# Window attention, max layer and gated layer: operand sums moved to VectorE, a raw-weight buffer and a new list order

## The chip, the cores and the metric

One core of a Trainium2 chip runs the whole program. The metric is the device time of one execution in microseconds. A core has five engines that run side by side, each through its own queue and in that queue's order: TensorE (PE, with its weight load PEld), VectorE (DVE), ScalarE (ACT), GpSimd (POOL) and SyncE (SP), which here issues nearly all DMA transfers.

## What is computed

Attention over a window of 32 with 32 global tokens, then a layer that takes the maximum of three products, then a gated layer; 2176 tokens of width 512 go through the two layers. The part that the change touches, cut:

```python
def _moe_ref(x, w1, w2, w3, w_out):                 # 512 -> 768 -> 512
    h = np.maximum(np.maximum(x @ w1, x @ w2), x @ w3)
    return h @ w_out

def _moe2_ref(x, w_gate, w_val, w_out):             # 512 -> 1536 -> 512
    gate = 1.0 / (1.0 + np.exp(-(x @ w_gate)))
    val = x @ w_val
    return gate * val @ w_out
```

The weights arrive as float64 and are converted on the chip from raw 32-bit halves.

## The kernel before

All SBUF work is laid out by hand and every step is a generator: one call of it issues one or a few instructions on given engines. `put` and `once` enter the steps with a nominal time into the list `ev`; `ORDER`, a list of numbers written out in the file, says in which order they are called. The order in which steps are called is the order of each engine's queue, and waits between engines follow from which memory a step reads and writes.

The stages overlap. Attention runs in 32 units up to about 400 us; the max layer ("first layer") runs in eight chunks of 256 or 288 tokens (`moe1_l1`, blocks f of the hidden width, three weights each, and `moe1_l2`), the last chunk, number 7, at 404 to 454 us, with its blocks in the order 2, 1, 0, 4, 3, 5. A hidden block needs a max by VectorE, a cast by ScalarE and the difference `h` by GpSimd (`sub`, line 269).

The gated layer multiplies by Strassen's scheme in its Winograd form: a *unit* (q, j, p) is gate or value (q = 0, 1), weight block j of six, token pair p of three; it has seven products (`l3_prod`, line 1021) of six matmuls, and 384 or 320 columns. Each operand is split in a high part (cast by ScalarE) and a low part (difference). `x_prep(p)` makes the seven token operands of a pair, `w_prep(q, j)` the seven weight operands of a block from raw columns: ScalarE and VectorE convert (`to_f32`, lines 283 to 292; 289 and 292 are VectorE's two conversion steps), then four sums (lines 984 to 992) and three differences (997, 1000, 1002). These sums and differences run on GpSimd for 8 of the 12 weight blocks, and 4 of 7 differences of `x_prep` (line 964) do, too. The products of one unit accumulate in the banks `pa`, `pb` and `pe`; between products ScalarE must copy the bank `pa` to `sn` (`snap`, line 1027) before PE may go on in it, so a snapshot that is late stops PE. `l3_out` then adds (line 1040, one operand in PSUM), applies the sigmoid or multiplies (line 1046, both operands in SBUF), and SP stores to `gd`.

PE runs a unit's products in the order 1, 5, 4 of the unit before, 6, 2, 3 of the unit before, 7. `wo_pre` converts `w_out` and stores it; `wo_prep(f)` loads and splits one block of it (lines 1068 to 1074), `g_prep(i)` loads and splits 128 tokens of the gated result (1082 to 1089), `moe2_l4` (1100) is the output product, `moe2_out` evicts and stores it.

Raw columns of weights go through two places, `AWR` and `AWR2`, which `w_prep` and `wo_pre` share. The first layer's weights lie in 26 slots of 4 KB a partition; when that layer has used them, slots 0 to 3.5 become the gated layer's first weight buffer, 3.5 to 7 the second, and 7 to 17.5 hold token pair 1.

Of the kernel before, what the change touches and what calls it, by code (L numbers as in the profile page):

```python
# [190 lines left out]
]  # L191

SLOT = {
# [9 lines left out]
def kernel(  # L203
# [61 lines left out]
    def f32(ap):  # L265
        return ap.bitcast(F32)
# [1049 lines left out]
```

## Time and profile before

| | |
|---|---|
| median of 3 runs | 863.91 us (862.85 to 868.32) |
| profiled execution | 865.5 us, span 863.8 us, mean granted clock 0.99 |
| PE / PEld busy | 95% / 87% of the span |
| DVE / ACT / POOL busy | 60% / 52% / 29% |
| chain that ended last | PE 71%, DVE 8%, DMA 8%, SP queue 5%, issue 4%, ACT 3%, POOL 1% |
| DMA | 109.73 MB, mean 127 GB/s |

The span is the time from the first to the last instruction of the profiled execution; its own time is 1.7 us longer. "Busy" is the time in which an engine executes; matmuls are pipelined, and their ends are modelled. Times in rows are from the start of the span.

### The profile page before, as it was taken

Reading aid. Unit: us, or ns where it says so; the run is one execution under the profiler, and the core shown is the slowest. Engines: PE = TensorE matmul, PEld = TensorE weight load, DVE = VectorE, ACT = ScalarE, POOL = GpSimd, SP = SyncE. Lnnn points to the kernel's source line nnn. Section 1 sums busy time; section 2 is a strip of 40 time slices with the busy share of each in tenths; the row PEclk is TensorE's granted clock in tenths of the full one; section 3 lists DMA queues with packets and bytes.
Section 4 is the critical chain, followed back from the end, with each engine's and each line's share of the span. In section 5 each row is a group of like instructions: output and inputs, shape, how many; then the busy total and the mean of one; then the engine's idle time right before and its main releaser. Section 6 shows DMA issues by size and latency. Waiting matters only on the chain.

```text
span 863.8 us, 17113 instructions
## 1 busy us (share of the span) xinstructions
PE 823.5 (95%) x6422; PEld 747.3 (87%) x6422; DVE 516.8 (60%) x1126; ACT 448.4 (52%) x1100; POOL 252.4 (29%) x223
## 2 busy tenths in 40 slices
PE   5899699999999999999998999999999999999998
PEld 3677589898998989899898999999999988888886
DVE  3969867757666576853776765667665557122120
ACT  4986456736555575563446645656564435222221
POOL 2142245234232433422542131544444012000000
PEclk9999799999999999999999999999999999999999
DMA  8967346444445455455223245536342157443430
GB/s 201 269 173 194 80 78 116 82 91 98 97 102 94 79 112 108 86 86 158 74 100 123 95 156 175 195 127 226 136 149 83 58 189 226 132 143 114 130 110 36
DMA packets 224707, 109.73 MB, mean 127 GB/s; under 512 B 160752, under 2 KB 209392, under 8 KB 224624
## 3 DMA queue, kind: packets, MB, share of 16 engines
q1 hardware_dynamic: 221968, 107.98, 46.7%
q8 instruction: 50, 0.82, 0.4%
q10 hardware_dynamic: 2656, 0.66, 0.4%
q14 instruction: 33, 0.27, 0.1%
HBM read 71.76 MB, written 25.43 MB: 113 GB/s over the span
## 4 chain that ended last, share of the span: by engine, by line
PE 71%; DVE 8%; DMA 8%; SPq 5%; issue 4%; ACT 3%; POOL 1%; DVEq 0%; ACTq 0%; POOLq 0%
PE acc L1100 16%; PE pa L1021 12%; PE ps L319 9%; PE ps L321 8%; PE ps L320 8%; PE pe L1021 5%; DMA m<-in_moe_w_dram 4%; PE pb L1021 3%; PE sp L611 2%; PE ot L765 2%; PE ps L903 2%; PE sg L628 1%; DVE m L292 1%; DVE m L289 1%; DMA m<-gd 1%
## 5 line engine op out<-in xcount | busy, mean ns | idle before, releaser
L1021 PE MATMUL pa<-m,m 128*128 128x384 f32 (+1 forms) x864 | 158.6, 331 | 10.2 <-ACT sn L1027 10.0
L1021 PEld LDWEIGHTS pa<-m,m 128*128 128x128 f32 x864 | 144.8, 189 | 15.2 <-ACT sn L1027 14.9
L319 PE MATMUL ps<-xt,m 128*128 128x288 f32 (+1 forms) x504 | 149.3, 296 | 3.1 <-DVE h L881 3.1
L321 PE MATMUL ps<-xt,m 128*128 128x288 f32 (+1 forms) x504 | 146.6, 291 | 0.0
L320 PE MATMUL ps<-xt,m 128*128 128x288 f32 (+1 forms) x504 | 145.0, 288 | 0.0
L1100 PE MATMUL acc<-m,m 128*128 128x512 f32 x612 | 139.1, 389 | 0.0
L1100 PEld LDWEIGHTS acc<-m,m 128*128 128x128 f32 x612 | 114.8, 188 | 23.8
L319 PEld LDWEIGHTS ps<-xt,m 128*128 128x128 f32 x504 | 94.7, 188 | 11.1 <-issue 4.5
L320 PEld LDWEIGHTS ps<-xt,m 128*128 128x128 f32 x504 | 94.8, 188 | 0.0
L321 PEld LDWEIGHTS ps<-xt,m 128*128 128x128 f32 x504 | 94.7, 188 | 0.0
L1089 DVE TENSOR_TENSOR m<-m,m 128x768 fp32r<-128x768 f32 x34 | 32.1, 977 | 90.0 <-ACT m L1087 89.9
L1021 PE MATMUL pe<-m,m 128*128 128x384 f32 (+1 forms) x432 | 83.1, 327 | 0.0
L1027 ACT COPY sn<-pa 128x384 f32<-128x384 f32 (+1 forms) x108 | 49.2, 458 | 58.3 <-PE pa L1021 53.5
L1021 PEld LDWEIGHTS pe<-m,m 128*128 128x128 f32 x432 | 73.2, 189 | 0.0
L881 DVE TENSOR_TENSOR h<-ps,h 128x288 f32<-128x288 f32 (+1 forms) x90 | 39.1, 437 | 53.2 <-PE ps L321 45.7
L646 ACT ACTIVATE sm<-sm,st 128x224 f32<-128x224 f32 x128 | 60.7, 477 | 9.6 <-DVE st L617 9.3
L1105 ACT COPY o<-acc 128x512 f32<-128x512 f32 x17 | 10.0, 587 | 102.5 <-issue 74.0
L269 POOL TENSOR_TENSOR h<-h,h 128x288 fp32r<-128x288 f32 (+1 forms) x42 | 37.0, 883 | 83.6 <-ACT h L886 78.0
L692 DVE TENSOR_TENSOR pc<-sm,pc 64x512 f16<-64x512 f32 (+1 forms) x72 | 51.5, 715 | 6.5 <-ACT pc L689 5.6
L269 POOL TENSOR_TENSOR m<-m,m 128x512 fp32r<-128x512 f32 x24 | 33.1, 1384 | 72.2 <-ACT m L310 46.3
L585 POOL TENSOR_TENSOR vr<-vr,vb 128x512 f32<-128x512 f32 x24 | 29.9, 1246 | 80.4 <-ACT vb L583 66.0
L617 DVE CUSTOM_DVE_ANT_0 sm<-sp,mask 128x224 f32<-128x224 f32 x128 | 43.8, 383 | 13.2 <-PE sp L611 10.6
(158 smaller groups left out, 1580.8 us busy)
## 6 DMA issues: line engine op xcount, KB each, us to landing
m<-gd SPq DMA_DIRECT2D x17, 768.0 KB, 4.9
m<-in_moe_w_dram SPq DMA_DIRECT2D x18, 512.0 KB, 6.2
gd<-sgt SPq DMA_DIRECT2D x48, 192.0 KB, 3.4
m<-in_moe_w_gate_dram SPq DMA_DIRECT2D x6, 1024.0 KB, 5.8
m<-in_moe_w_val_dram SPq DMA_DIRECT2D x6, 1024.0 KB, 6.0
m<-in_moe_w_out_dram SPq DMA_DIRECT2D x6, 1024.0 KB, 5.2
vr<-in_v_l_dram SPq DMA_DIRECT2D x48, 96.0 KB, 2.5
out_dram<-o SPq DMA_DIRECT2D x17, 256.0 KB, 2.0
```

The costliest lines, as they stand in the source:

```text
L269: nc.gpsimd.tensor_tensor(out=out, in0=a, in1=f32(b), op=ALU.subtract)
L319: nc.tensor.matmul(ps, lhsT=wh, rhs=xh, start=first, stop=False)
L320: nc.tensor.matmul(ps, lhsT=wh, rhs=xl, start=False, stop=False)
L321: nc.tensor.matmul(ps, lhsT=wl, rhs=xh, start=False, stop=last)
L617: nc.vector.tensor_tensor_reduce(out=sm[:, hh, j], in0=sp[hh][:, j, 0:224], in1=mask[:, half + j, :], scale=-SC, scalar=3.0e38, op0=ALU.ad ...
L646: nc.scalar.activation(sm4[:, i], sm4[:, i], AF.Exp, bias=st[:, 0, i:i + 1], scale=-1.0, accum_out=st[:, 2, i:i + 1])
L692: nc.vector.tensor_tensor(out=l_, in0=s_, in1=h_, op=ALU.subtract)
L881: nc.vector.tensor_tensor(out=a, in0=ps[:, 0:n], in1=a, op=ALU.max)
L1021: nc.tensor.matmul(ps, lhsT=w[l][:, a, i], rhs=x[m][:, i], start=(k in (1, 2, 5) and i + l + m == 0), stop=(k in (2, 3, 4) and i == 1 and ...
L1027: nc.scalar.copy(t[:, 0:n], pend[u]["a"][:, 0:n])
L1089: nc.vector.tensor_tensor(out=lo, in0=a, in1=f32(hi), op=ALU.subtract)
L1100: nc.tensor.matmul(acc[i], lhsT=t[l][:, f % 6], rhs=w[m], start=(f == 0 and l + m == 0), stop=(f == NF2 - 1 and l == 1))
```

## The change

- `x_prep`, `w_prep` and `wo_prep`: all sums and differences go to VectorE; GpSimd keeps those of the first layer.
- `w_prep`: the cast of the four sums is issued in two halves.
- A third place for raw columns: a tile `wr` in the pool that holds `sgt`. `wo_pre` and the block (0, 1) use it; `AWR` and `AWR2` are then left to the other blocks.
- `SLOT`: the slots of `w` and `raw` of the first layer are permuted. Each group of tenants that shared a slot still shares one: blocks 2, 1, 0 now lie in slots 0 to 2, 3 to 5, 6 to 8, blocks 4, 3, 5 in 9 to 11, 12 to 14, 15 to 17.
- `tm` has two buffers in place of three; the output tile `o` lies where the weight buffers were.
- `ORDER` and the nominal times: the first 1918 entries, up to the last chunk's first product, name the same steps; from there the list is new. It has 24 more entries, two for each `w_prep`. In it `x_prep(0)` runs ahead of the conversion of the first gate block; the loads of `wo_prep` are issued one by one during the units (1, 5, 0) and (1, 5, 1), where they stood behind the former's last product; the load of gate block 2 is issued before those of `x_prep(2)`; and `g_prep`'s first casts stand after product 4 of unit (0, 5, 2).

The diff without the lists:

```diff
 SLOT: ("kx", 1): 11 -> 14, ("vrg", 0, 0): 7 -> 1
-SLOT.update({("raw", i): n for i, n in enumerate(
-    (9, 8, 21, 2, 10, 1, 19, 13, 17, 12, 23, 14, 16, 15, 18, 20, 25, 24, 6, 13, 17, 12, 23, 21))})
-SLOT.update({("w", i): i for i in range(24)})
+for k, n in (("raw", (12, 2, 21, 8, 13, 7, 19, 10, 17, 9, 23, 11, 16, 15, 18, 20, 25, 24, 0, 10, 17, 9, 23, 21)),
+             ("w", (6, 7, 8, 3, 4, 5, 0, 1, 2, 12, 13, 14, 9, 10, 11, 15, 16, 17, 18, 19, 20, 21, 22, 23))):
+    SLOT.update({(k, i): s for i, s in enumerate(n)})
...
 x_prep
-            eng = nc.gpsimd if op in (B11, T2, T3, B22) else nc.vector
-            eng.tensor_tensor(out=v[1], in0=a, in1=f32(v[0]), op=ALU.subtract)
+            nc.vector.tensor_tensor(out=v[1], in0=a, in1=f32(v[0]), op=ALU.subtract)
...
-    def w_prep(q, j, buf, at, fast):
+    def w_prep(q, j, buf, at):
-        raw = mem(at, (KD * 2 * P, 2), I32)
+        if at:
+            raw = mem(at, (KD * 2 * P, 2), I32)
+        else:
+            raw = sg_pool.tile([P, KD * 2 * P, 2], I32, tag="wr", name="wr", bufs=1)
...
-        eng = nc.vector if fast else nc.gpsimd
-        tt = eng.tensor_tensor
+        tt = nc.vector.tensor_tensor
...
-        nc.scalar.copy(hi[:, S1:S4 + 1], lo)
-        yield
+        for o in (0, 2):
+            nc.scalar.copy(hi[:, S1 + o:S1 + o + 2], lo[:, o:o + 2])
+            yield
...
 l3_out
-            c = d if q == 0 else rb.tile([P, CH], F32, tag="tm", name="tm", bufs=3)[:, 0:n]
+            c = d if q == 0 else rb.tile([P, CH], F32, tag="tm", name="tm", bufs=2)[:, 0:n]
 wo_pre
-        raw = mem(at, (2 * DM, 2), I32)
+        raw = sg_pool.tile([P, 2 * DM, 2], I32, tag="wr", name="wr", bufs=1)
 wo_prep
-        (nc.gpsimd if f % 2 else nc.vector).tensor_tensor(out=lo, in0=v, in1=f32(hi), op=ALU.subtract)
+        nc.vector.tensor_tensor(out=lo, in0=v, in1=f32(hi), op=ALU.subtract)
 moe2_out
-        o = rb.tile([P, DM], F32, tag="o", name="o", bufs=3)
+        o = mem(DM * (i % 3), (DM,))
...
-    jobs = [(0, 0, 0, AWR, T_ATT + .1, 424.0), (1, 0, 1, AWR, 429.5, 0), (0, 1, 0, AWR, 458.0, ended[(0, 0, 2), 3] + .3)]
-    free = {AWR: ended[(0, 0, 2), 3] + 8.5, AWR2: 466.0}
+    jobs = [(0, 0, 0, AWR, T_ATT + .2, 0), (1, 0, 1, AWR, 421.5, 0), (0, 1, 0, 0, 456.0, ended[(0, 0, 2), 3] + .3)]
+    free = {AWR: 458.0, AWR2: 466.0}
```

## Rows read from the trace of the kernel before

**Rows 1.** busy time by stretch: length, each engine (instructions), granted clock, DMA share, GB/s

```profile
420.00:454.00 34.00, 31.46 (x229) 30.79 (x230) 24.90 (x30) 15.45 (x28) 15.58 (x11) 1.00 0.28 95
454.00:500.00 46.00, 42.21 (x238) 40.63 (x238) 33.70 (x49) 27.67 (x51) 9.09 (x5) 0.96 0.32 107
...
542.00:584.00 42.00, 41.70 (x251) 41.07 (x251) 27.64 (x39) 25.43 (x44) 22.50 (x17) 1.00 0.50 170
...
710.00:732.00 22.00, 19.66 (x94) 16.99 (x93) 15.25 (x20) 12.47 (x23) 6.29 (x5) 0.92 0.78 254
...
sum 464.00, PE 447.02 PEld 416.84 DVE 236.80 ACT 205.38 POOL 114.74; mean PE 44.70 PEld 41.68 DVE 23.68 ACT 20.54 POOL 11.47
```

**Rows 2.** TensorE's waits from 400 us: total, times, longest, us

```profile
PE pa L1021 <- ACT sn L1027: 10.0, 12, 2.0
PE ps L319 <- DVE h L881: 2.1, 2, 2.0
PE ps L320 <- POOL h L269: 0.7, 1, 0.7
```

**Rows 3.** busy time around two stretches at a low clock, columns as in rows 1

```profile
458.00:462.00 4.00, 3.93 (x14) 3.93 (x14) 2.14 (x1) 1.78 (x3) 1.05 (x1) 0.57 0.41 107
462.00:470.00 8.00, 8.00 (x48) 8.00 (x48) 4.84 (x6) 3.95 (x8) 1.98 (x1) 1.00 0.79 279
700.00:709.00 9.00, 9.00 (x59) 9.00 (x58) 5.95 (x11) 3.81 (x8) 1.82 (x2) 1.00 0.82 246
713.00:719.00 6.00, 5.57 (x26) 5.05 (x25) 3.69 (x7) 4.24 (x10) 2.32 (x2) 0.72 1.09 367
```

**Rows 4.** groups of VectorE by shape, 400 to 732: count | busy, mean ns | idle before

```profile
L1046 DVE TENSOR_TENSOR sgt<-tm,sgt 128x384 f32<-128x384 f32 x36 | 30.1, 835 | 1.0
L292 DVE SCALAR_TENSOR_TENSOR m<-m 128x1024 int32<-128x1024 int32 x18 | 26.4, 1464 | 0.1
L289 DVE SCALAR_TENSOR_TENSOR m<-m 128x1024 int32<-128x1024 int32 x18 | 25.2, 1398 | 10.0 <-ACT m L287 9.9
...
L997 DVE TENSOR_TENSOR m<-m,m 128x512 fp32r<-128x512 f32 x4 | 2.8, 692 | 2.7 <-ACT m L994 2.7
...
L992 DVE TENSOR_TENSOR m<-m,m 128x256 f32<-128x256 f32 x4 | 1.7, 418 | 0.0
```

**Rows 5.** single VectorE instructions: duration ns min/median/max, first and last start

```profile
L289 DVE SCALAR_TENSOR_TENSOR m<-m x18: 1217/1227/3190, 415.8 to 657.7; 128x1024 int32<-128x1024 int32 x18
...
L1046 DVE TENSOR_TENSOR sgt<-tm,sgt x54: 485/559/2127, 478.3 to 730.9; 128x384 f32<-128x384 f32 x36, 128x320 f32<-128x320 f32 x18
L1040 DVE TENSOR_TENSOR tm<-pe,sn x36: 482/546/560, 481.0 to 729.6; 128x384 f32<-128x384 f32 x24, 128x320 f32<-128x320 f32 x12
```

**Rows 6.** groups of GpSimd by shape, 400 to 732, columns as in rows 4, one group

```profile
L269 POOL TENSOR_TENSOR h<-h,h 128x288 fp32r<-128x288 f32 x6 | 5.6, 926 | 13.9 <-ACT h L886 8.4 <-issue 5.5
```

**Rows 7.** timeline at 513 us: start, length, engine and line, idle before

```profile
513.25 2.40 POOL L1002 TENSOR_TENSOR m<-m,m 128x1024 fp32r<-128x1024 f32 x1
...
513.54 3.19 DVE L289 SCALAR_TENSOR_TENSOR m<-m 128x1024 int32<-128x1024 int32 x1 [4.87 <-ACT m L287]
...
518.64 1.14 PE L1021 MATMUL pa<-m,m 128*128 128x384 f32 x5 [1.65 <-ACT sn L1027]
```

**Rows 8.** timeline at 417 us of VectorE and TensorE

```profile
417.52 2.75 DVE L292 SCALAR_TENSOR_TENSOR m<-m 128x1024 int32<-128x1024 int32 x1
420.19 0.95 DVE L964 TENSOR_TENSOR m<-m,m 128x768 fp32r<-128x768 f32 x1
...
419.32 0.28 PE L321 MATMUL ps<-h,m 128*128 128x256 f32 x1
421.56 0.40 PE L319 MATMUL ps<-xt,m 128*128 128x288 f32 x1 [1.97 <-DVE h L881]
```

**Rows 9.** timeline at 711 us of ScalarE and TensorE

```profile
711.26 0.83 ACT L1087 CAST m<-m 128x768 fp32r<-128x768 f32 x1 [2.86 <-DMA m<-gd]
...
712.47 1.15 PE L1021 MATMUL pa<-m,m 128*128 128x320 f32 x6 [1.91 <-ACT sn L1027]
```

More of the change, by code (lines that the diff above doesn't have):

```diff
@@ L113 @@
     1740, 1225, 1294, 1226, 1737, 1739, 1295, 1296, 1297, 1298, 1308, 1309, 1729, 1750, 1310, 1311, 1741, 1742, 1312,
[77 rows of a table removed]
[78 rows of a table added]
 ]
 SLOT = {
-    ("qn", 0): 15, ("kx", 0): 25, ("kn", 0): 22, ("qn", 1): 20, ("kx", 1): 11, ("kn", 1): 18, ("vrg", 0, 0): 7,
+    ("qn", 0): 15, ("kx", 0): 25, ("kn", 0): 22, ("qn", 1): 20, ("kx", 1): 14, ("kn", 1): 18, ("vrg", 0, 0): 1,
     ("vrg", 0, 4): 4, ("vrg", 1, 0): 24, ("vrg", 1, 4): 22,
 }
-SLOT.update({("raw", i): n for i, n in enumerate(
-    (9, 8, 21, 2, 10, 1, 19, 13, 17, 12, 23, 14, 16, 15, 18, 20, 25, 24, 6, 13, 17, 12, 23, 21))})
-SLOT.update({("w", i): i for i in range(24)})
+for k, n in (("raw", (12, 2, 21, 8, 13, 7, 19, 10, 17, 9, 23, 11, 16, 15, 18, 20, 25, 24, 0, 10, 17, 9, 23, 21)),
+             ("w", (6, 7, 8, 3, 4, 5, 0, 1, 2, 12, 13, 14, 9, 10, 11, 15, 16, 17, 18, 19, 20, 21, 22, 23))):
+    SLOT.update({(k, i): s for i, s in enumerate(n)})
 @with_exitstack
@@ L993, in w_prep @@
         yield
-        nc.scalar.copy(hi[:, S1:S4 + 1], lo)
-        yield
+        for o in (0, 2):
+            nc.scalar.copy(hi[:, S1 + o:S1 + o + 2], lo[:, o:o + 2])
+            yield
         low = mem(3584 * buf + 1792, (7, 2, P), F32R)
+        w7[q, j] = hi, low
         tt(out=low[:, A11:A12 + 1].rearrange("p o k f -> p (o k) f"), in0=h[:, :, 0],
@@ L1002, in w_prep @@
         tt(out=low[:, S1:S4 + 1], in0=lo, in1=f32(hi[:, S1:S4 + 1]), op=ALU.subtract)
-        w7[q, j] = hi, low
         yield
@@ L1051, with wo_pre @@
     wo = {}
-    def wo_pre(i, at):
-        raw = mem(at, (2 * DM, 2), I32)
+    def wo_pre(i):
+        raw = sg_pool.tile([P, 2 * DM, 2], I32, tag="wr", name="wr", bufs=1)
         nc.sync.dma_start(out=raw.rearrange("p (f d) t -> p f (d t)", f=2),
@@ L1059, in wo_pre @@
         yield from to_f32(raw, True, out=c)
-        c = f32(c)
         yield
-        nc.sync.dma_start(out=wod[2 * i:2 * i + 2].rearrange("f p d -> p f d"), in_=c.rearrange("p (f d) -> p f d", f=2))
+        nc.sync.dma_start(out=wod[2 * i:2 * i + 2].rearrange("f p d -> p f d"), in_=f32(c).rearrange("p (f d) -> p f d", f=2))
         yield
@@ L1195, in end_moe1 @@
     def end_moe1():
-        nonlocal sgt
+        nonlocal sgt, sg_pool
         xh_x.close()
@@ L1200, in end_moe1 @@
         post.append(sg_x)
-    rb = sgt = ps_b = None
+    rb = sgt = sg_pool = ps_b = None
     post = []
@@ L1236 @@
         for f, t, t0 in ((0, 0, ended[v, 2] + .25), (1, 1, ended[v, 7] + .7), (0, 1, ended[v, 3] + .25)):
-            put(("l3o", *v, f, t), steps(t0, 0, .7, 1.5), l3_out(v, f, t))
+            put(("l3o", *v, f, t), steps(t0, 0, .7 if v[0] else 1.5, 1.5), l3_out(v, f, t))
         put(("l3o", *v, 1, 0), steps(ended[v, 4], .2, 1.5), l3_out(v, 1, 0))
-    for p, tm in ((0, T_ATT + .2), (1, 426.0), (2, 450.8)):
-        first = (7.0, 7.0, 3.5)[p]
-        put(("xp", p), steps(tm, 0, first, *(3 * (.8,)), *(14 * (.6 if p == 2 else .8,))), x_prep(p))
+    for p, tm, first in ((0, T_ATT + .3, 8.5), (1, 424.0, 8.0), (2, 450.8, 3.5)):
+        put(("xp", p), steps(tm, 0, first, *(3 * (1.25 if p == 1 else .9,)), *(14 * (.6 if p == 2 else .8,))), x_prep(p))
     AWR2 = AXR
-    jobs = [(0, 0, 0, AWR, T_ATT + .1, 424.0), (1, 0, 1, AWR, 429.5, 0), (0, 1, 0, AWR, 458.0, ended[(0, 0, 2), 3] + .3)]
-    free = {AWR: ended[(0, 0, 2), 3] + 8.5, AWR2: 466.0}
+    jobs = [(0, 0, 0, AWR, T_ATT + .2, 0), (1, 0, 1, AWR, 421.5, 0), (0, 1, 0, 0, 456.0, ended[(0, 0, 2), 3] + .3)]
+    free = {AWR: 458.0, AWR2: 466.0}
     for n in range(3, 2 * (NF2 // 2)):
@@ L1249 @@
         jobs.append((q, j, q, AWR2 if n % 2 else AWR, None, ended[(q, j - 1, 2), 3] + .3))
-    n_wo = 0
     for q, j, buf, place, t0, ready in jobs:
@@ L1253 @@
             t0 = free[place]
-            if (q, j) != (1, 1) and n_wo < NF2 // 2:
-                put(("wo", n_wo), steps(t0, 0, 9.0, 1.2, 1.2, 1.3, 1.3), wo_pre(n_wo, place))
-                n_wo += 1
-                t0 += 15.5
-            free[place] = ready + 8.5
-        fast = (q, j) in ((0, 1), (1, NF2 // 2 - 1)) or j == 0
-        first = steps(t0, 0, 9.0, 1.2, 1.2, 1.3)
-        gaps = (.1, .4, .4, .4, .4, .4, .6, .4) if fast else (.1, .7, .7, .7, .7, .7, 1.3, .7)
-        put(("w7", q, j), first + steps(max(ready, first[-1] + 1.2), *gaps), w_prep(q, j, buf, place, fast))
-    assert n_wo == NF2 // 2
+        first = steps(t0, 0, 9.0, 1.2, 1.2, 1.3)
+        go = max(ready, first[-1] + 1.4)
+        if j > 1 or (q, j) == (1, 1):
+            free[place] = go + 7.5
+        put(("w7", q, j), first + steps(go, *(.1, .45, .45, .45, .45, .6, .6, .8, .6, 1.2)), w_prep(q, j, buf, place))
+    for i in range(NF2 // 2):
+        put(("wo", i), steps(490.0 + 28 * i, 0, 9.0, 1.2, 1.2, 1.3, 1.3), wo_pre(i))
     v0 = ended[(1, NF2 // 2 - 1, 0), 3]
@@ L1267 @@
     for f in range(NF2):
-        put(("wop", f), steps(v0 + .3 + .9 * f, 0, 4.0, .8), wo_prep(f))
+        put(("wop", f), steps(v0 + .3 + 1.1 * f, 0, 4.0, .8), wo_prep(f))
     for i in range(NT // P):
```

155 rows, old and new, of the table ORDER are left out of this document.

## The prediction

> **What bounds the kernel now.** I read the page first, then the busy time by stretch, then TensorE's waits, then the timelines of VectorE, ScalarE and GpSimd around each wait. On the page TensorE (PE) is busy 95% of the span and the chain that ended last is 71% PE. The diff leaves the first 1918 of the listed steps in place, that is, everything up to about 405 us, and its new slots there only swap numbers: each slot's tenants stay together, so every wait in that part stays. What can change lies after 400 us. From there to the end PE is busy 447.0 of 464 us [rows 1], the final eviction and store included in the rest. The matmuls that PE runs are the same before and after, so the only thing to win is the time PE stands still or runs slowly.
>
> That time is small and can be counted. PE waits 10.0 us in 12 places for ScalarE's snapshot `sn` of the bank `pa`, 2.1 us for a VectorE max `h`, and 0.7 us for a GpSimd difference `h` [rows 2]: 12.8 us. Each wait costs about 0.15 us more than its idle time, because the idle time starts only when the last matmul's pipeline has drained (1.97 us is listed in [rows 8] where the starts lie 2.24 us apart and some 0.12 is usual for 256 columns); 15 waits make 2.3 us. Behind two waits the granted clock falls: 0.57 in 458 to 462, where 14 matmuls start instead of the 24 that fit in 4 us of the next row, and 0.72 in 713 to 719 [rows 3], both a mix of the level at 1.2 and the one at 2.4 GHz, and in both PE had stood still for about 2 us just before. The first costs 10 x 0.167 = 1.7 us, the second (39 would fit at the rate of 700 to 709, 26 start, 0.43 us of it idle) 13 x 0.153 - 0.43 = 1.6 us. In all 12.8 + 2.3 + 1.7 + 1.6 = 18.4 us, 2.1% of the span. It is the most that any edit here can give back.
>
> Why does PE wait for a short copy? ScalarE works in order and stands behind something that waits for VectorE or GpSimd. At 513.25 GpSimd begins a 1024-wide difference of 2.40 us; VectorE's conversion step begins 0.3 us later and takes 3.19 us, PE then stands for 1.65 us [rows 7]. The same instruction has a minimum of 1217 ns and a median of 1227 [rows 5]. So a VectorE operation that meets a GpSimd one is held until that one ends. It holds for operations that read two SBUF tensors: the multiply L1046 ranges from 485 to 2127 ns, while the add L1040, of the same width with one operand in PSUM, never exceeds 560 [rows 5]. At 417.5 the step takes 2.75 us, and the max behind it lets PE stand 1.97 us [rows 8].
>
> **The change part by part.**
>
> *Operand sums from GpSimd to VectorE* (`x_prep`, `w_prep`, `wo_prep`). GpSimd loses 12 differences of `x_prep`, 7 operations in each of 8 `w_prep` jobs, and 6 of `wo_prep`; of its 114.7 us after 400 only the `h` differences, 5.6 us in the last row, remain [rows 1, 6]. On VectorE the prices are: 0.95 us for 768 columns when nothing collides [rows 8], so 8 x 0.95 + 4 x 0.81 (640 columns, scaled) = 10.8 us; for a `w_prep` job four sums and one difference of 256 at 0.42, one of 512 at 0.69 [rows 4], one of 1024 at 1.22 (no quiet row; the other 1024-wide two-input operation [rows 5]) = 4.0 us, so 32.1 us for eight; 6 x 0.69 = 4.1 us for `wo_prep` (512 columns). Added: 47 us. Against it VectorE gets back what the collisions cost: L1046 36 x (835 - 559) = 9.9 us, L292 18 x (1464 - 1224) = 4.3 (median taken from its twin, 1227), L289 18 x (1398 - 1227) = 3.1 [rows 4, 5], and smaller ones that together I put at the same rate, 17 + 10 = 27 us. Net VectorE gains about 20 us of work over 330 us. Where it lies: 454 to 500 is the fullest, 33.7 of 46 us now [rows 1]; there it loses about 5 us of collisions (a fifth of the 27), gets 5 sums (4.2 us) and a conversion pulled ahead (2.4 us), so some 35 in a stretch that should be 42 long, 84%. In the middle, 27.6 of 42 [rows 1] becomes 27.6 - 4 + 8 = 31.6, 75%. VectorE does not become the bound; the sums lie beside PE's products. If that cover were gone, the 20 us would be the price.
>
> *What the waits become.* The max at 421 us: the new order puts all of `x_prep(0)` and all but one of the maxes it meets ahead of the two conversion steps, so the max that PE waits for stands behind 0.95 us differences only. I followed VectorE from the first sum of `x_prep(0)` with the prices above: it reaches each max before PE needs the bank, and the 2.1 us go. What is late next is the last hidden block `h` of the first layer, which needs max, cast and GpSimd difference in a row: I keep 0.5 of the 0.7 us. The longest wait for `sn`, 2.0 us [rows 2], stands just ahead of 458: the GpSimd difference that held the conversion there is gone and the weight casts end before the first product, so it and the 1.7 us of low clock behind it go. The later ones have their cause in [rows 7] and go with it, except where the new order still leaves ScalarE a queue before a snapshot.
>
> *The third raw buffer.* `w_gate`'s and `w_out`'s raw columns get a tile of their own, so loads start earlier. DMA is at 0.28 to 0.50 of its engines in the stretches of [rows 1] before 710, and a load that starts earlier is hidden by PE's work; no PE wait after 400 names a DMA [rows 2]. SP issues the same count of transfers, but in one place a load moves ahead: the 1 MB of gate block 2 now stands on SP's queue before the four loads of `x_prep(2)`. At 279 GB/s [rows 3] it takes 3.7 us. The stores that those four wait for come about 4 us earlier, because the copies of the first layer's last blocks no longer stand behind the late casts of the value block, so I take 0; without that cover VectorE would start `x_prep(2)` up to 3.7 us later, and PE would see what exceeds its 2 us of slack, 1.7 us.
>
> *The tail.* At 711.26 ScalarE has waited 2.86 us for the first load of `g_prep`, with a snapshot behind it: PE waits 1.91 us [rows 9] and another 0.43 after 713 [rows 3], in a stretch where DMA is at 0.78 [rows 1]. The new order issues the 12 `wo_prep` loads 8 to 12 us earlier (8 to 12 products of about 1 us), each as soon as its operand's product is done, and puts the `g_prep` cast some 7 us of products behind its load. The 2.3 us and the low clock go. But two casts of 0.83 us [rows 9] and a third stand before the second snapshot of the last unit, with 2.6 us of products to cover them: I keep 0.9 us.
>
> *The rest.* The cast of the four sums is split in two: one instruction more per block on a ScalarE that is 60% busy [rows 1], and the first half starts earlier: 0. Buffers `tm` from 3 to 2: written and read by VectorE alone, in order: 0. The output tile `o` in another place: the copy is the same: 0. If a region there were released late, one such copy would be exposed.
>
> *Slots of the first layer.* The first slots to be released are now those the gated layer's first buffer wants (its blocks are used in the order 2, 1, 0, 4, 3, 5, and block 2 now lies in slots 0 to 2). Operands may be written some 3 us earlier; PE waits for none now, so 0 by itself, but it is what lets the order above hold.
>
> **The sum.** 18.4 us less what I expect to stay: 0.5 (`h`), 0.9 (tail), 0.8 where the second gate block `w7(0,1)` is ready only as its product begins (seven VectorE steps and two casts in 7.5 us of products), 1.5 for short snapshot waits of 0.2 to 0.3 us in the five remaining blocks, and 0.15 x 8 = 1.2 for draining; 4.9 us stay. Gain 13.5 us. The profiled execution took 865.5 us with a span of 863.8, so 852.0 by its own time; the median of the runs is 1.6 us lower, 863.9, and so I predict 850.5 us.
>
> **The rivals.**
>
> 1. *Half of it comes back* (0.18). VectorE, at 84% in 454 to 500 and fuller still in the 30 us before, where both token pairs and both weight blocks are made, is late with sums; ScalarE's casts wait for them in order, and the snapshot behind them is late again. For it: ScalarE has such waits now. Against: without collisions no VectorE operation exceeds 1.23 us, and a snapshot has about 2 us of products as slack. Place: 420 to 500; price about half of the 18.4 us plus what stays: gain 7, 857 us.
>
> 2. *No difference* (0.10). The waits have another cause than the collisions, and the list order only moves them: 861 to 867, 864 us. For it: PE's work is untouched at 95% of the span. Against: the held instruction and the wait stand in the same microseconds [rows 7, 8]. The Trainium skill (Perfetto Trace Analysis, Identifying the Most-Contended Engine) says to work on the engine with the highest occupancy; by that rule, read plainly, a change to VectorE and GpSimd would leave this time where it is.
>
> 3. *Slower* (0.05). VectorE is too full, and the adds that empty the banks come late in every unit. It decides from the point where a unit's VectorE work exceeds its products, 42 matmuls or 7 us at the rate of 462 to 470 [rows 3]; the sum above has 75 to 84%. Price: one 0.9 us wait in each of 36 units less the 18.4 us, 32 - 18 = +14, 878 us. The Trainium skill (Perfetto Trace Analysis, Optimizing Scalar/DVE Operations) advises offloading a saturated VectorE, to GpSimd too, and this change does the reverse; it adds that the two share a port so that offloading may not help, and the trace bears out the second half: L1046's 2127 ns.
>
> **How the numbers follow.** The forecast has 0.67: 846 to 855 us on its own. About 1% (8.6 us) is what a measurement of this kernel tells from no change. Faster by over 1% is below 855.3: the forecast and about half of rival 1, 0.77; within 1%: the rest of it and rival 2, 0.18; slower: rival 3, 0.05. The range reaches down to 844.5, where all 18.4 us and a little more go, and up to 859.5, where rival 1 takes its full price: some 0.8 lies inside.
>
> **What would show it.** Right: after 400 us GpSimd has only the `h` differences; L289 and L292 stay near 1.22 us and L1046 near 0.56; PE's waits for `sn` fall from 10.0 to about 3 us; the granted clock stays at its upper level after the first gated product and in the tail; the first gated product begins about 3 us earlier than now, and the first product of the output layer 13 us earlier than now. Up to 400 us nothing moves. Wrong: VectorE above 90% in 454 to 500 with PE waiting for `sn` or for a bank there (rival 1 or 3), collisions gone and waits still there (rival 2), or a PE wait that names a DMA.

## The result

The changed kernel takes 843.85 us (median of 4 runs, 843.43 to 845.62), the kernel before, beside it on the same chip, 863.9 us (862.85 to 868.32): a ratio of 0.976, 95% interval 0.973 to 0.980. The forecast was 850.5 us in a range from 844.5 to 859.5. The direction and the mechanism came out as foreseen, the size did not: 20.05 us were won where 13.5 were forecast.

The profiled execution's span is 842.0 us, 21.8 less than before. 1.9 us of that lie ahead of 400 us, where both kernels call the same steps; in eleven profiles of this study with the changed kernel's list up to there, the attention ended between 399.1 and 402.5 us, so this part is scatter from one execution to the next. Behind it 19.9 us were won.

Busy time by stretch, changed kernel, columns as in [rows 1]:

```profile
420.00:454.00 34.00, 33.41 (x242) 33.17 (x241) 27.81 (x39) 18.85 (x34) 6.56 (x6) 1.00 0.34 106
454.00:500.00 46.00, 46.00 (x277) 45.70 (x277) 35.69 (x60) 30.74 (x57) 0.00 (x0) 1.00 0.45 161
542.00:584.00 42.00, 42.00 (x256) 42.00 (x255) 29.17 (x52) 24.79 (x47) 0.00 (x0) 1.00 0.54 179
...
688.00:735.00 47.00, 46.65 (x231) 40.26 (x230) 19.39 (x28) 16.81 (x27) 0.00 (x0) 1.00 0.62 180
```

PE is busy without a break in the second and third row, at the upper of its two clock levels (2.4 GHz), where [rows 1] had 42.2 of 46 and 41.7 of 42 us. The fourth row holds the last gated products and the first of the output layer, with the granted clock at its upper level too. VectorE stands at 35.7 of 46 us (78%) and 29.2 of 42 (69%); GpSimd does nothing from 450 us on. TensorE's waits from 400 us, against [rows 2]:

```profile
PE ps L321 <- POOL h L270: 0.6, 1, 0.6
PE pa L1024 <- ACT sn L1030: 0.3, 1, 0.3
```

Twelve waits for `sn` have become one, and the two for a max are gone. Single VectorE instructions of the changed kernel from 400 to 735 us (duration in ns min/median/max), against [rows 5] (L290, L293 and L1049 were L289, L292 and L1046):

```profile
L290 DVE SCALAR_TENSOR_TENSOR m<-m x11: 1212/1226/1229, 419.6 to 635.1; 128x1024 int32<-128x1024 int32 x11
...
L293 DVE SCALAR_TENSOR_TENSOR m<-m x11: 1216/1219/1470, 421.1 to 636.7; 128x1024 int32<-128x1024 int32 x11
...
L1049 DVE TENSOR_TENSOR sgt<-tm,sgt x54: 491/557/560, 467.3 to 708.8; 128x384 f32<-128x384 f32 x36, 128x320 f32<-128x320 f32 x18
```

The conversion step that reached 3190 ns reaches 1229, the multiply that reached 2127 reaches 560. The medians were the same before: only the held ones have gone. (The conversions that now work in the tile `wr`, seven for each line, are not in these rows; they take 1.22 us as well.)

### The profile page after: what moved, and what is told of

Same layout as the page of the kernel before. It is cut to its first block, busy times and chain, and to the rows that moved or that the text cites. A ratio compares the mean times of both kernels' runs of the same rounds, so it can differ in the third digit from the quotient of the medians.

```text
span 842.0 us, 17071 instructions
## 1 busy us (share of the span) xinstructions
PE 815.9 (97%) x6422; PEld 744.4 (88%) x6422; DVE 529.8 (63%) x1200; ACT 452.1 (54%) x1112; POOL 148.5 (18%) x149
## 4 chain that ended last, share of the span: by engine, by line
PE 85%; DVE 5%; DMA 4%; SPq 2%; ACT 2%; issue 1%; POOL 0%; POOLq 0%; DVEq 0%; ACTq 0%
PE pa L1024 17%; PE acc L1102 16%; PE ps L320 10%; PE ps L322 9%; PE ps L321 9%; PE pe L1024 8%; PE pb L1024 4%; PE sp L612 3%; PE ot L766 2%; PE ps L904 2%; PE sg L629 1%; DMA m<-in_moe_w_dram 1%; DMA m<-in_v_l_dram 1%; PE ps L868 1%; PE og L835 1%
## 5 line engine op out<-in xcount | busy, mean ns | idle before, releaser
L1024 PE MATMUL pa<-m,m 128*128 128x384 f32 (+1 forms) x864 | 155.1, 327 | 0.3 <-ACT sn L1030 0.3
L1089 ACT CAST m<-m 128x768 fp32r<-128x768 f32 x34 | 28.5, 840 | 83.9 <-PE acc L1102 71.7
L882 DVE TENSOR_TENSOR h<-ps,h 128x288 f32<-128x288 f32 (+1 forms) x90 | 39.0, 437 | 43.6 <-PE ps L322 36.7
L270 POOL TENSOR_TENSOR h<-h,h 128x288 fp32r<-128x288 f32 (+1 forms) x42 | 41.4, 988 | 97.1 <-ACT h L887 93.1
L320 PE MATMUL ps<-h,m 128*128 128x288 f32 (+1 forms) x168 | 50.4, 300 | 0.0
L321 PE MATMUL ps<-h,m 128*128 128x288 f32 (+1 forms) x168 | 48.5, 289 | 0.6 <-POOL h L270 0.6
```

The source lines that it names most:

```text
L270: nc.gpsimd.tensor_tensor(out=out, in0=a, in1=f32(b), op=ALU.subtract)
L320: nc.tensor.matmul(ps, lhsT=wh, rhs=xh, start=first, stop=False)
L321: nc.tensor.matmul(ps, lhsT=wh, rhs=xl, start=False, stop=False)
L882: nc.vector.tensor_tensor(out=a, in0=ps[:, 0:n], in1=a, op=ALU.max)
L1024: nc.tensor.matmul(ps, lhsT=w[l][:, a, i], rhs=x[m][:, i], start=(k in (1, 2, 5) and i + l + m == 0), stop=(k in (2, 3, 4) and i == 1 and ...
```

## The experiments

Two things may have made the gain, and the prediction had them in one account: the sums' engine (theory 1: collisions of GpSimd with VectorE; theory 2: GpSimd's results only come late) and the list (theory 3). Where the text below says "the new list", the slots, the third raw buffer, the other buffers and the split cast come with it. All runs are compared with the kernel before on their own chip, whose medians were 862.1 to 864.5 us. For the stages, lengths are read from the starts of PE's matmuls: the last matmul of the attention (E), the first gated product (G), then every 252 matmuls of the gated layer, which is one gate and one value block (each boundary lies two products behind the first product of gate block j), and the first output product (O). From O to the last matmul all kernels take 140.3 us. Each row is one profiled execution; for "new list, sums on GpSimd" it was the longest of the four, 856.95 us where the median is 853.55.

| us from the profiled execution | E to G | j 0 | j 1 | j 2 | j 3 | j 4 | j 5 to O | sum |
|---|---|---|---|---|---|---|---|---|
| before | 52.6 | 48.7 | 45.9 | 42.5 | 42.2 | 42.3 | 44.1 | 318.2 |
| old list, sums on VectorE | 52.2 | 46.8 | 42.4 | 41.8 | 41.8 | 41.8 | 43.6 | 310.4 |
| new list, sums on GpSimd | 52.4 | 45.6 | 42.6 | 45.7 | 41.6 | 41.6 | 40.7 | 310.3 |
| new list, weight blocks alone on GpSimd | 49.4 | 42.2 | 42.4 | 43.3 | 41.6 | 41.6 | 40.0 | 300.6 |
| new list, token pairs alone on GpSimd | 52.4 | 45.7 | 41.8 | 41.6 | 41.6 | 41.6 | 40.4 | 305.1 |
| changed | 49.4 | 42.2 | 41.8 | 41.6 | 41.6 | 41.6 | 40.1 | 298.3 |
| changed, second profile | 49.4 | 42.2 | 41.8 | 41.6 | 41.6 | 41.6 | 39.4 | 297.7 |

**The engine alone.** The kernel before with

```diff
-            eng = nc.gpsimd if op in (B11, T2, T3, B22) else nc.vector
+            eng = nc.vector
...
-        eng = nc.vector if fast else nc.gpsimd
+        eng = nc.vector
...
-        (nc.gpsimd if f % 2 else nc.vector).tensor_tensor(out=lo, ...
+        nc.vector.tensor_tensor(out=lo, ...
```

> The kernel before with its own list, slots and buffers; only the engine of the gated layer's sums and differences is changed, all of them on VectorE. If the collisions of GpSimd with VectorE made the waits (theory 1), VectorE's conversion steps fall to a maximum near 1.25 us, PE's snapshot waits after 400 us fall from 10.0 to 2 to 4 us, and the time is 850 to 855 us. If only the results on GpSimd were slow in coming and nothing was held (theory 2), the time is about the same 850 to 855, so this kernel does not tell 1 from 2. If the new list made the gain (theory 3), the waits move little and the time is 860 to 866 us.

856.9 us, ratio 0.993 (0.991 to 0.995): 7.1 us, a third of the gain, between the ranges of the theories. The collisions are gone (no conversion step is above 1.23 us), the snapshot waits fall to 6.4 us, not to 2 to 4. What is left is the old list. Timeline of VectorE and TensorE at 416 us in this kernel (start, length, engine and line, idle before):

```profile
416.10 1.22 DVE L289 SCALAR_TENSOR_TENSOR m<-m 128x1024 int32<-128x1024 int32 x1
417.35 1.23 DVE L292 SCALAR_TENSOR_TENSOR m<-m 128x1024 int32<-128x1024 int32 x1
418.50 1.82 DVE L964 TENSOR_TENSOR m<-m,m 128x768 fp32r<-128x768 f32 x2
420.23 0.45 DVE L881 TENSOR_TENSOR h<-ps,h 128x288 f32<-128x288 f32 x1
...
420.74 0.40 PE L319 MATMUL ps<-xt,m 128*128 128x288 f32 x1 [1.72 <-DVE h L881]
```

Nothing here is held, and PE still stands 1.72 us (1.97 in [rows 8]): four steps of their normal length are listed ahead of the max that PE needs.

**The list alone.** The changed kernel with the same three lines put back (GpSimd for what it did before).

> The changed kernel with its list, slots and buffers; only the sums and differences that the change moved go back to GpSimd. Theories 1 and 2: most of the gain is lost, 856 to 864 us, snapshot waits of 6 to 12 us, conversion steps of up to 3 us under theory 1 and of 1.22 us under theory 2. Theory 3 (the list made the gain): 845 to 850 us.

853.55 us, ratio 0.990 (0.987 to 0.993): 10.5 us, half of the gain, between what the theories said. TensorE's waits from 400 us:

```profile
PE pa L1026 <- ACT sn L1032: 5.0, 4, 2.3
PE ps L320 <- DVE h L882: 1.7, 1, 1.7
PE pe L1026 <- DVE m L965: 1.2, 1, 1.2
...
```

The 1.7 us are those at 421 us, now for the other reason. Timeline of VectorE, GpSimd and TensorE:

```profile
418.69 3.72 DVE L965 TENSOR_TENSOR m<-m,m 128x768 fp32r<-128x768 f32 x2
422.33 2.87 DVE L290 SCALAR_TENSOR_TENSOR m<-m 128x1024 int32<-128x1024 int32 x1
425.12 0.45 DVE L882 TENSOR_TENSOR h<-ps,h 128x288 f32<-128x288 f32 x1
...
415.74 4.37 POOL L965 TENSOR_TENSOR m<-m,m 128x768 fp32r<-128x768 f32 x2 [0.96 <-ACT m L962]
...
425.62 0.40 PE L320 MATMUL ps<-xt,m 128*128 128x288 f32 x1 [1.73 <-DVE h L882]
```

The list has one step ahead of the max, but it takes 2.87 us. So this stall had two sufficient causes, and the first column of the table shows it whole: engine alone 0.3 us, list alone 0.2 us, both 3.1 us. In block 1 it is the other way round, either alone wins 3.3 to 3.5 of 4.1 us; in block 2 the new list with the old engines loses 3.2 us (2.3 of it in one wait at 547 us, taken up under *Which sums*). In the last stage the list alone wins 3.4 of 4.1.

**Which sums.** The changed kernel with `w_prep` alone, then with `x_prep` alone, on GpSimd as before.

> The changed kernel with only the eight weight blocks' sums and differences back on GpSimd; the token operands and the output weights stay on VectorE. If the stall around the first gated product comes from the token differences on GpSimd beside the conversion, the first gated product is as early as in the changed kernel (448.8 us) and what is lost lies in gate blocks 1 to 5: 848 to 853 us, about 5 to 9 us lost. If the weight blocks are not what collides, 844 to 846 us.

> The changed kernel with only four of the seven differences of each token pair back on GpSimd (12 instructions of 768 or 640 columns). With all sums back 10.5 us were lost, with the weight blocks alone 2 to 4. If the rest is the token pairs: 848 to 852 us, the first gated product about 3 us later and unit 1 slower, as with all sums back. If only both groups together lose it: 844 to 847 us.

846.3 us (0.982, 0.980 to 0.983) and 852.4 us (0.986, 0.984 to 0.988). The second ran beside the changed kernel (844.1 us): 8.3 us lost, 6.5 of them in the first two stages. Twelve `x_prep` instructions on GpSimd cost PE three times what 56 of `w_prep` cost, and they stand in 414 to 484 us, where VectorE is fullest; that this is the reason is argued, not shown. What the trace does show is that the three longest of the waits with `x_prep` alone on GpSimd (1.7, 1.3 and 1.2 us, at 425, 456 and 476 us) stand behind VectorE steps that were held: conversions of 2.85 and 2.87 us where 1.22 is usual, and a difference of 1.96 us where 0.82 is.

The wait in block 2 with `w_prep` alone on GpSimd takes a longer way. Timelines of GpSimd, VectorE, SP and ScalarE in that kernel (L1050 is the multiply, L1059 the load of raw `w_out` columns into the tile `wr`):

```profile
523.35 2.79 POOL L1007 TENSOR_TENSOR m<-m,m 128x1024 fp32r<-128x1024 f32 x1
...
524.38 2.18 DVE L1050 TENSOR_TENSOR sgt<-tm,sgt 128x384 f32<-128x384 f32 x1
526.48 1.21 DVE L293 SCALAR_TENSOR_TENSOR m<-wr 128x1024 int32<-128x1024 int32 x1
...
528.14 0.46 SPq L1059 DMA_DIRECT2D wr<-in_moe_w_out_dram  x1
...
537.05 1.13 ACT L284 ACTIVATE wr<-wr 128x1024 uint32<-128x1024 uint32 x1 [3.98 <-DMA wr<-in_moe_w_out_dram]
```

A difference on GpSimd holds a multiply, which takes 2.18 us instead of 0.56; the conversion behind it empties `wr` late, the next load into `wr` starts late, ScalarE waits 4.0 us for it, and PE stands 1.4 us for a snapshot behind that. With all sums on GpSimd the same chain (a multiply of 2.18 us again, 4.8 us of waiting) makes the 2.3 us at 547 us. So holding reaches PE through the third raw buffer, too. By the profiles the two kernels lose 9.0 us together and the one with all sums back 11.9, but that last execution was 3.4 us longer than its median; by the medians it loses some 9.7 us, about what the two lose together. (The 10.5 us of the expectation above is what the list alone wins.)

**The slots alone.** The kernel before with the new `SLOT`.

> The kernel before with the permuted slots of the first layer's operands alone. All theories: no change, 863 to 865 us, since PE waited for none of the operands that a freed slot would let in earlier. If the slots change what runs before 400 us (the changed kernel's profile reached the end of the attention 1.9 us earlier), the time is 862 us and that stretch is shorter here too.

863.7 us, ratio 1.000 (0.998 to 1.002). The permutation is worth nothing by itself. Its profile ends the attention at 399.4 us as the changed kernel's does, but its median is that of before: one more sign that the 1.9 us are scatter. The reverse, the new list on the old slots, wasn't tried: a weight operand would be written before the slot's last reader is called. For a like reason the third raw buffer wasn't taken away alone: the new list loads gate block 2 while the block before is still being read.

**The collision by itself.** The changed kernel, with GpSimd busy on something nobody needs:

```diff
+        def tt(**kw):
+            vt(**kw)
+            if spare is not None and len(n_sum) < 4:
+                n_sum.append(1)
+                for _ in range(3):
+                    nc.gpsimd.tensor_tensor(out=spare, in0=a21, in1=a22, op=ALU.add)
```

> The changed kernel, and beside it GpSimd adds two SBUF operands of 256 columns 96 times in the gated layer (12 for each of eight weight blocks), into a scratch that nobody reads. No result of the computation comes from it. Theory 1 (GpSimd's reads hold VectorE): VectorE's conversion steps or sums beside them grow to over 1.5 us, its products L1049 above 0.8 us in places, and 2 to 8 us of the gain are lost: 846 to 852 us. Theory 2 (only GpSimd's late results cost): 843 to 845 us, no VectorE duration moves.

867.7 us, ratio 1.004 (1.002 to 1.006): 96 idle additions take back the whole gain and more, so far more than I expected. No result of the computation comes from GpSimd in the gated layer here, so theory 2 cannot be the whole account; holding alone is enough to stop PE. One group, one wait, and a timeline of this kernel:

```profile
L995 POOL TENSOR_TENSOR spare<-m 128x256 bf16<-128x256 f32 x96 | 103.8, 1082 | 107.1 <-PE pe L1035 53.8 <-DVE m L293 46.2
```

```profile
PE pa L1035 <- ACT sn L1041: 15.8, 14, 2.3
```

```profile
499.93 12.24 POOL L995 TENSOR_TENSOR spare<-m 128x256 bf16<-128x256 f32 x10
...
501.22 3.90 DVE L991 TENSOR_TENSOR m<-m,m 128x512 fp32r<-128x512 f32 x3 [1.09 <-ACT m L1008]
...
505.04 1.86 DVE L290 SCALAR_TENSOR_TENSOR wr<-wr 128x1024 int32<-128x1024 int32 x1
...
506.83 0.54 DVE L1054 TENSOR_TENSOR sgt<-pb,sn 128x384 f32<-128x384 f32 x1
...
507.41 0.52 ACT L1057 ACTIVATE sgt<-sgt 128x384 f32<-128x384 f32 x1 [4.45 <-DVE sgt L1054]
...
508.35 3.70 PE L1035 MATMUL pa<-m,m 128*128 128x384 f32 x12 [2.25 <-ACT sn L1041]
```

Read from the bottom: PE stands 2.25 us for a snapshot, which stands behind a sigmoid on ScalarE, which has waited 4.45 us for VectorE's adds, which stand behind three differences and a conversion that took 3.90 and 1.86 us instead of 2.3 and 1.22, beside GpSimd's burst. The add with one operand in PSUM takes its usual 0.54 us. This is the chain that the prediction read from [rows 7], made on purpose. The Trainium skill (SBUF — State Buffer, SBUF: two separate sides) states that the port which the two engines share is an exclusive lock held for a whole instruction, and that a VectorE operation contends when it has two SBUF inputs and GpSimd's reads SBUF; the durations in this timeline agree.

Not all of the 24 us are held VectorE operations. Of the 16.8 us of TensorE's waits from 480 us on, 3.3 (1.6 at 517, 0.6 at 523 and 1.1 at 548 us) stand behind conversions on ScalarE that wait for a load of raw columns. The first of these loads waited on SP's queue for the idle additions, which read the place that it writes:

```profile
SPq L974 <- POOL spare L995: 6.0, 1, 6.0
```

**Theory 2 in the kernel before.** Followed back in its trace, the twelve waits for `sn`, 10.0 us, have several causes: 5.9 us in seven waits stand behind a VectorE instruction of over its usual length, 2.3 us in the last two behind the loads of `g_prep`, 0.8 us in two behind steps of their usual length, and 0.9 us, at 540 us, behind a cast that waited 2.6 us for a GpSimd sum. ScalarE's waits for these sums in that kernel, 400 to 735 us (of the eight, that one ends directly ahead of the snapshot that PE waits for):

```profile
ACT m L994 <- POOL m L992: 8.7, 8, 2.6
```

So theory 1 has the larger part, and theory 2 is not nothing.

**Copies instead of additions**, once 96 and once 192 (`range(6)`):

```diff
-                    nc.gpsimd.tensor_tensor(out=spare, in0=a21, in1=a22, op=ALU.add)
+                    nc.gpsimd.tensor_copy(out=spare, in_=a21)
```

> As the run with 96 idle additions on GpSimd (which cost 24 us), but each idle operation copies one SBUF operand of 256 columns in place of adding two. Its place, its waits and the memory it reads are the same; no result of the computation comes from it. If the second SBUF operand on GpSimd is what holds VectorE: VectorE's durations as in the changed kernel, 843 to 846 us. If any GpSimd access does, or if the idle work costs through raw columns that come free later: 855 to 868 us again.

> As the run with idle copies on GpSimd, with 192 copies in place of 96, so that GpSimd is busy about as long (103 us) as in the run with 96 idle additions (104 us), which held VectorE for 31 us from 450 us on and PE for 22 us; 96 copies held VectorE for 9 us and PE for 3. If holding goes by GpSimd's busy time: VectorE held for 18 us or more, 850 to 860 us. If it goes by what GpSimd's operation reads: much less per busy time than additions; VectorE held for 10 to 18 us, 846 to 851 us.

847.2 us (0.982, 0.981 to 0.984) and 857.9 us (0.993, 0.991 to 0.994; the changed kernel beside it 844.1). So a GpSimd copy with one SBUF operand holds VectorE too. From 450 to 735 us I summed, for each kind of VectorE instruction, the time above its tenth percentile: 1.4 us in the changed kernel, 9.2 with 96 copies (51 us of GpSimd), 14.0 with 192 (107 us), 30.8 with 96 additions (104 us). For equal busy time additions hold VectorE more than twice as much. PE's loss in the doubled run is not all holding: 8.2 of its 14.6 us are one stall at 514 us, which starts with a load of raw columns that waits on SP's queue for the spare copies to let go of the place (9.5 us in all, 8.5 the longest, where the additions made it wait 6.0):

```profile
DVE m L290 <- POOL spare L995: 9.4, 1, 9.4
ACT m L284 <- DMA m<-in_moe_w_val_dram: 9.2, 1, 9.2
```

The same load comes late in the run with additions, but there ScalarE waits 2.8 us for it and PE 1.6. So the 14.0 us of held time fit the second expectation, and the time fits neither.

**The last stage.** The changed kernel with `wo_prep`'s steps (12 loads of 256 KB, casts, differences) between the products where the list of before has them.

> The changed kernel with the steps of the output weights (12 loads, casts and differences) at the places between products which they have in the kernel before; all else as changed. If the early loads made the gain of the last stage (43.6 us with the old list and all sums on VectorE, 40.1 as changed), the stretch from the last gate block to the first output product grows by 3 to 4 us with PE waiting for a snapshot in it: 846.5 to 848 us. If the stage gained only by the missing collisions, no change: 843 to 845 us.

852.8 us, ratio 0.988 (0.986 to 0.990). The stage grows from 40.1 to 47.5 us, twice what I expected, in one wait of 5.7 us. Timeline of ScalarE:

```profile
692.41 0.47 ACT L1047 ACTIVATE sgt<-sgt 128x320 f32<-128x320 f32 x1
698.67 0.62 ACT L1074 CAST m<-m 128x512 fp32r<-128x512 f32 x1 [5.79 <-DMA m<-wod]
```

Issued together, the loads take 4.8 us each to land, 3.0 as changed. ScalarE stands before a cast, and the snapshot of the last unit stands behind it. Moving the loads forward carries this stage, and the rest of the new list needs it: with the old places the stage takes 47.5 us in the new list and 43.6 in the old.

**The split cast undone.** The cast of the four sums as one instruction, at the second half's place.

> The changed kernel with the four sums of a weight block cast by one ScalarE instruction again, at the place of the second half. The prediction put the split at nothing. If so: 843 to 845 us and PE's wait for sn stays at 0.3 us. If the shorter cast is what lets snapshots through in time: snapshot waits of 1 to 3 us in the gate blocks, 845 to 847 us.

845.1 us, ratio 0.978 (0.975 to 0.981): no difference in time. The profiled execution was the longest of its four, 849.3 us (the others 844.2 to 845.5). Its trace has snapshot waits of 2.1 us in two places: 1.0 us at 540 us, where the changed kernel has none, and 1.1 in the last stage, where other runs of the same steps have 0 to 1.3. It also has 0.4 us at 493 us for a VectorE difference that comes late behind the longer cast. The wait at 540 us stands behind the same conversion from `wr` as above: counted from the first gated product, its load is issued 0.8 us later than in the changed kernel (PE itself is 0.4 us behind by then), and lands after 8.7 us where 7.8 and 7.1 are seen there. Whether the split is worth this 1 us is not settled by one profile.

**The last `h` on VectorE.**

```diff
-            sub(h[:, 1, 0:n], a, h[:, 0, 0:n])
+            (nc.vector if c == NC - 1 else nc.gpsimd).tensor_tensor(out=h[:, 1, 0:n], in0=a, ...
```

> The changed kernel with the difference h of the first layer's last chunk (six blocks of 288 columns) on VectorE in place of GpSimd. After the change PE still stands 0.75 us at 440 us for the last such difference on GpSimd, whose six take 1.68 us each beside a VectorE that is 82% busy. If GpSimd's length sets that wait: no wait for it, 0.4 to 0.8 us less, which the trace can show and the time cannot; first gated product 0.4 to 0.8 us closer to the end of the attention. If VectorE has no room there, a max comes late: PE waits for DVE h, 1 to 2 us more.

845.3 us, ratio 0.977 (0.975 to 0.979). The wait for GpSimd's `h` is gone and the first stage is 48.9 us instead of 49.4; in this execution the last stage had a wait of 1.3 us for a snapshot, so the sum shows nothing.

**Is VectorE ever too full?** The changed kernel with the first layer's 24 differences (line 313, 20 to 145 us) on VectorE too.

> The changed kernel with the differences of the first layer's 24 weight operands (512 columns each) on VectorE too, where the changed kernel leaves them to GpSimd. It tests the rival by which VectorE is too full. From 20 to 100 us VectorE is busy 74 to 99%; 24 times 0.69 us is 16.5 us more, less the collisions there (9 us in 20 to 125 us). If a full VectorE delays PE: slower by 4 to 12 us, 848 to 856 us, all of it before 130 us. If the collisions are worth as much as the work here too: 842 to 846 us.

851.4 us, ratio 0.984 (0.982 to 0.986), where the two kernels before it in this text took 845.1 and 845.3 on the same chip: 6.2 us slower. So the same move loses here. Stretches of this kernel and a wait of TensorE in it:

```profile
20.00:100.00 80.00, 68.95 (x492) 54.61 (x490) 76.45 (x204) 64.38 (x190) 3.49 (x3) 0.99 0.76 196
...
125.00:145.00 20.00, 16.78 (x159) 15.11 (x158) 15.20 (x45) 9.17 (x25) 6.09 (x6) 1.00 0.46 72
```

```profile
PE ps L322 <- DVE m L313: 3.2, 1, 3.2
```

and the same stretches as changed:

```profile
20.00:100.00 80.00, 68.27 (x484) 53.94 (x481) 73.62 (x191) 63.28 (x187) 24.18 (x18) 0.98 0.74 195
...
125.00:145.00 20.00, 20.00 (x220) 18.21 (x219) 14.12 (x39) 12.88 (x33) 11.97 (x11) 1.00 0.60 102
```

VectorE goes from 92 to 96% in 20 to 100 us, though the collisions of 20 to 125 us fell from 9.0 to 3.4 us; a weight's difference comes late, and PE stands 3.2 us for it at 137 us, in a stretch where it stood not at all. The rest of the loss is in no single wait. A share is no threshold, though: in the changed kernel PE loses nothing in ten microseconds in which VectorE is full.

```profile
414.00:424.00 10.00, 10.00 (x81) 10.00 (x80) 9.97 (x14) 4.64 (x10) 5.92 (x2) 1.00 0.40 127
```

**A version that beats both.** The longest stall left in the changed kernel lies outside the change: at 91 us PE waits 5.9 us for a conversion (L293) of the first layer's output weights on VectorE. First I gave three of its steps to ScalarE (`LOW_ACT_A` with 19, 21, 23), then I moved four of them ahead of softmax steps in the list.

> The changed kernel, and beyond the change one step (the low word's scaling, 128 by 512) of three of the first layer's output weight blocks goes from VectorE to ScalarE, in the stretch 60 to 100 us, where VectorE is busy over 97% and PE stands 5.9 us for a conversion on it, while ScalarE is busy 57 to 74%. If VectorE's load sets that stall, 2 to 4 us are won: 840 to 842 us. If the stall moves to ScalarE's queue, no change, 843 to 845 us.

> The changed kernel with four conversion steps of the first layer's output weights (512 columns each on VectorE) some 10 to 80 places earlier in the list, ahead of softmax steps, in 85 to 95 us; all else as changed. PE stands 5.9 us at 91 us for the last of them, the longest stall that is left in the kernel. Moving three low words from VectorE to ScalarE did not shorten it (5.9 us before, 6.5 after). If the order on VectorE sets it: 2 to 4 us less, 840 to 842 us. If VectorE's load sets it, the stall comes back at the softmax steps behind: 843 to 847 us.

> The changed kernel itself, as the measure for the other runs on this chip: 843 to 846 us. After 400 us its waits are 0.6 us for GpSimd's h and 0.3 to 1.5 us for a snapshot in the last stage.

> The version with four conversion steps of the first layer's output weights earlier in the list, again, beside the changed kernel on the same chip: 840 to 842 us, 2 to 4 us below it.

Less work did nothing: 844.6 us (0.980, 0.978 to 0.981), and the wait is still there at 92 us, 6.2 us long. The earlier place did: 840.9 us (0.972, 0.970 to 0.974), and again 840.9 us (0.974, 0.971 to 0.976) beside 844.1 us for the changed kernel (0.977, 0.975 to 0.979), 3.2 us less. TensorE's waits from 60 to 130 us, as changed and in this version:

```profile
PE ps L904 <- DVE m L293: 5.9, 1, 5.9
PE ps L868 <- DVE m L293: 1.4, 1, 1.4
PE ps L904 <- issue: 1.3, 1, 1.3
```

```profile
PE ps L905 <- ACT sm L648: 2.3, 1, 2.3
PE ps L905 <- DVE m L294: 1.9, 1, 1.9
PE ps L869 <- DVE m L294: 1.3, 1, 1.3
```

## Why the prediction was right or wrong

**The ceiling was mis-sized: 18.4 us, where 22.1 stood there.** The prediction called the 18.4 us the most that any edit after 400 us can give back, and 20.05 were won. Summed from start to start over all of PE's matmuls from 400 to 840 us, the time above the usual pitch was 22.1 us before; it is 1.9 after, and 1.4 in the second profile. The prediction built its ceiling from the list of waits and added draining and low clock. Two terms were missing. The first matmul behind a stall costs more as well:

```profile
421.80 0.30 PE L320 MATMUL ps<-xt,m 128*128 128x288 f32 x1
421.93 0.30 PE L321 MATMUL ps<-xt,m 128*128 128x288 f32 x1
```

(Kernel before, timeline of TensorE.) The one ahead of these is the first behind a stall, at 421.56 in [rows 8]; the next starts 0.24 us after it, and from then on the pitch is 0.13: 0.11 us more, behind each of some 19 stalls, 2.0 us. And the list leaves out stalls of 0.16 to 0.29 us, five of them, 1.1 us. Small steps make up the rest.

**What was kept was mis-sized: 4.9 us, where 1.9 stayed.** The `h` was right (0.5 kept, 0.75 with its draining there). The tail kept 0.9; it shows 0.5 as changed, nothing in the second profile, up to 1.5 with draining in other runs of the same steps: of the right size. The 0.8 for the second gate block, the 1.5 for short snapshot waits in the middle and most of the 1.2 for draining were caution without a row: no matmul from 454 to 690 us is more than 0.15 us late. (22.1 - 18.4) + (4.9 - 1.9) = 6.7 us, about the 6.5 us by which the forecast fell short.

**Right, and shown:** that VectorE's two-input operations are held by GpSimd's (30.8 us of it with the idle additions, which cost 24 us); that the larger part of the waits for `sn` is made by that through ScalarE's queue (5.9 of 10.0 us; the tail's 2.3 us come from loads, as predicted); that both stretches of low clock go with the stalls ahead of them (granted 1.00 in every row of the result, the tail included, 0.57 and 0.72 in [rows 3]); that the max at 421 us needs the list too; that VectorE does not become the bound (78% where 84% were forecast, 69% where 75%). After 400 us VectorE has 249.8 us of work where [rows 1] had 236.8: 13 more, not 20. The lengths of its instructions add up to 18 more, but back to back they overlap (five of 0.95 us in 4.42). No wait of PE names a DMA, and `x_prep(2)`'s first sum begins 9.5 us after the first gated product, where it began 10.6 after it before: gate block 2's earlier load costs nothing, as taken.

**Wrong in the account:** the prediction gave each stall one cause, let the list help here and there, and gave all snapshot waits outside the tail the cause of [rows 7]; 1.7 us of them had another (a late GpSimd sum, steps of their usual length). The two single runs win 7.1 and 10.5 us, and both at once 20.05: some 2.4 us of it come only with both. At the first gated product it is 2.6 of the 3.1.

**The landmarks:** first gated product 5.0 us earlier, 3.1 without the scatter ahead of it (3 forecast, right); first output product 21.8 earlier, 19.9 without it (13 forecast).

**The rivals.** Half coming back would have shown as `sn` waits at a VectorE near 90%; there is none from 420 to 500 us, with VectorE at 82 and 78% in the two rows, and the one that is left, 0.3 us, lies in the tail at 696 us. No difference is refuted: work on engines at 60% and 29% moved the time by 20 us. The Trainium skill's rule (Perfetto Trace Analysis, Identifying the Most-Contended Engine) to optimize the engine with the highest occupancy first would have misled here only if read as leaving the other engines alone: that engine, PE, lost its 22.1 us mostly in the others' queues. Slower did not happen in the gated layer, but a VectorE that comes late with a difference does cost time elsewhere: in 20 to 145 us the same move loses 6.2 us.

## What to carry to other kernels

A stall can have two sufficient causes, so try an engine change and a list change together and each alone before one of them is called useless. Count what stalls cost by the starts of the stalled engine's instructions, not by its list of waits: here 12.8 us of waits were listed and 22.1 lost, with draining, the slow first instruction, short stalls and the low clock. Moving two-input work off GpSimd won where VectorE ended at 78% of a stretch and lost where it stood at 92% before; the share alone does not decide, so look for the first result that PE needs and that would come late. And follow a wait to its start before naming its cause: behind the same line, a snapshot that is late, stood held instructions, loads and a late sum.

## What was not expected of the hardware

Holding goes both ways, and GpSimd can lose for several instructions on end. In the changed kernel's last chunk GpSimd's difference `h` takes 0.90 us in one place and 5.01 us in another, beside a run of VectorE's two-input operations (timelines of GpSimd and VectorE):

```profile
416.47 5.01 POOL L270 TENSOR_TENSOR h<-h,h 128x288 fp32r<-128x288 f32 x1 [11.81 <-ACT h L887]
422.33 0.90 POOL L270 TENSOR_TENSOR h<-h,h 128x288 fp32r<-128x288 f32 x1 [0.85 <-ACT h L887]
```

```profile
415.25 4.42 DVE L964 TENSOR_TENSOR m<-m,m 128x768 fp32r<-128x768 f32 x5
419.60 1.22 DVE L290 SCALAR_TENSOR_TENSOR m<-m 128x1024 int32<-128x1024 int32 x1
```

It ends 0.66 us after the last of six two-input operations that VectorE ran without a gap. This is one place, and PE did not wait for it; but a GpSimd instruction that PE needs can be late because VectorE is busy, not because GpSimd is. It is no rule that the engine without gaps loses nothing: of the ten additions at 499.93 us above, which ran without a gap, each took 1.22 us on average where the shortest of the 96 took 0.84, and VectorE's differences beside them were slowed too.
